# A gated mix of a long convolution and an MLP on one core: the same 1183 operations in another written-out order

## The chip, the cores and the metric

The kernel runs on one core of a Trainium2 chip. The time is device microseconds of one execution of the whole program, weights and activations read from HBM and the result written back to HBM. TensorE (PE) multiplies matrices, VectorE (DVE) and ScalarE (ACT) work on tiles of 128 partitions in SBUF and PSUM, GpSimd (POOL) does small arithmetic and issues DMAs that accumulate, and SyncE (SP) issues the other DMAs. Each engine takes its own instructions in the order in which they were written, and waits at semaphores for the others.

## The reference

One sequence of S = 2048 rows and D = 640 columns in bfloat16; F = 1536. `A_q` is both the query of branch A and the input of branch B.

```python
def _A_ref(q, k, v, shift_k, ssm_k, ssm_D):
    for t in range(ks):                      # 4 taps
        k_shift = k_shift + k_pad[:, t:t + S, :] * shift_k[:, ks - 1 - t]
    kv = k_shift * v
    y = irfft(rfft(kv padded to 2S) * rfft(ssm_k padded to 2S))[:S]
    y = y + kv * ssm_D
    return q * y

def _B_ref(x, w1, w2, w3, w4):
    h = gelu(layernorm(x) @ w1)
    hs = concat(four groups of columns of h, shifted by +1, -1, +2, -2 rows) @ w2
    x1 = x + hs
    return x1 + gelu(layernorm(x1) @ w3) @ w4

x = A_q
g = sigmoid((x * gate_w).sum(-1, keepdims=True))
return g * _A_ref(x, ...) + (1 - g) * _B_ref(x, ...)
```

(Shortened; the padding and the transposes are left out.)

## The kernel before

The kernel is written in two steps. First, functions such as `ln1`, `mm1`, `mm2`, `h_chunk`, `unit` and `final` record operations in the class `Prog` (line 175): each has an index from 0 to 1182, an engine, and the operations that it depends on. One operation can hold several instructions (a group of matmuls into one PSUM tile, a pass with an accumulator). Helpers record them, so the profile shows the helper's line: `mm` (L647) for matmuls, `act` (L637), `tt` (L627), `ts` (L632), `pool_pow` (L815), `Prog.dma` (L238). Second, `schedule` (line 255) puts the operations in the order of the list `SEQUENCE` (line 460), and each engine's and each DMA queue's instructions follow that order. The list `PLACES` (line 521) gives the first PSUM bank of each of 205 PSUM tiles; when a tile opens in a bank, its first operation waits for the operations other than PE's that used the tile before it there. `emit` (line 276) turns the dependences into semaphore waits. Nothing is decided at run time: both lists were written out ahead.

The stages, with the names of the groups that the text uses:

- Start: 15 warm-up matmuls (L675) on a tile that a DVE memset (L671) fills, and 26 fill matmuls (L679) that compute nothing the output needs. `x_load` brings rows of `A_q`; operations 73 to 76 load row tiles 0 to 3. `ln1` takes mean and variance on DVE (L811, L812), raises to the power -1/2 on POOL (L815), applies both on DVE, transposes on PE (L866, row tiles 0 to 7), and copies the transposed tile out of PSUM on ACT.
- `mm1` multiplies by w1 in pieces. ACT applies gelu while it evicts each piece into `hT`. The fifth piece of a chunk holds the last 32 columns of the four shift groups, so it is evicted in four pieces of 32 partitions, at partitions 0, 32, 64 and 96, each with its own shift. `mmg` computes the gate's products, `mm2` multiplies by w2 with the shift in the address, and the residual is added on DVE (L919) or on PE.
- `ln_math` and `ln2` are the second layer norm. For row tiles 4 to 15 the mean, power and the multiply of the two are 128x1 operations on POOL, and ACT applies them. `ln_math-15-16` (operations 580 to 585) belongs to row tile 15; 584 is its power, 585 its multiply, 586 the apply.
- `h_fold` and `h_chunk` transform the filter `ssm_k`, `kv_chunk` makes kv, `x_fwd` transforms it: folded DFTs as matmuls, evicted mostly by ACT. `combine` and `unit` form the spectral products on DVE (products of 128x2560), some of them added by accumulating DMAs on POOL's queue (798, 810, 968, 970 among them).
- `mm3` (w3, gelu on ACT) and `mm4` (w4) finish branch B; 895 to 916 are mm4 of row tiles 8 to 11, of which 897 evicts tile 8.
- `final` runs 16 times, `final-hh-c-q-k` with half of the columns hh: an inverse transform on PE, an ACT copy, a sum and a difference on DVE, a matmul with a flip matrix, an ACT eviction, then two or more DVE operations and the store. Its two row tiles go out in one store of 160 KB for k up to 13 and in two of 80 KB for k = 14 and 15. It is the last work of the kernel.

Of the kernel before, what the change touches and what calls it, by code (L numbers as in the profile page):

```python
# [422 lines left out]
def bass_gated_mix__ssm_conv_h3__mixer_s_mlp__prompt_kernel(  # L423
# [32 lines left out]
    def ps(n, cls):  # L456
# [3 lines left out]
    SEQUENCE = [76, 11, 56, 74, 54, 9, 1, 12, 75, 5, 4, 53, 7, 13, 8, 0, 73, 10, 14, 156, 15, 157, 16, 57, 60, 17, 81,  # L460
# [59 lines left out]

# [645 lines left out]
```

## Time and profile before

| | us |
|---|---|
| median of 3 runs | 231.58 (231.22 to 231.77) |
| profiled execution | 233.02 |
| its span, first to last instruction | 231.2 |
| PE busy | 219.1 (95%) |
| DVE busy | 206.8 (89%) |
| ACT busy | 175.3 (76%) |
| POOL busy | 96.3 (42%) |
| mean granted TensorE clock | 0.993 |

Busy time counts instructions that run, not the semaphores, branches and DMA issues. Weight loads of PE overlap its matmuls. Ends of matmuls are modelled and spans on POOL are rough, so differences of tenths of a microsecond on single POOL rows say little. A wait's releaser is inferred from semaphore events; `A <- B` reads "A waited for B".

### The profile page before, as it was taken

The page shows a single profiled execution, that of the slowest core. Times are in us where ns is not written, and L with a number is a line of the kernel's source. Part 1 is how long each engine was busy: PE and PEld are TensorE (multiplying, and loading weights), DVE is VectorE, ACT ScalarE, POOL GpSimd, SP SyncE. Part 2 cuts the span into 40 slices and gives each one's busy share as a digit, 9 for nine tenths or more (in the row PEclk, how much of TensorE's full clock was granted, in tenths as well). Part 3 has the DMA queues.
Part 4 walks back from the last instruction along what each step waited for, and adds up shares of the span by engine and source line. Part 5 has one row for each costly group of instructions (what it writes and reads, how often), then busy time and mean ns, then how long its engine had stood idle before and what let it go on. Part 6 is the DMA issues. An engine that isn't in the chain of part 4 may idle for free.

```text
span 231.2 us, 3878 instructions
## 1 busy us (share of the span) xinstructions
PE 219.1 (95%) x1437; PEld 127.0 (55%) x1437; DVE 206.8 (89%) x339; ACT 175.3 (76%) x315; POOL 96.3 (42%) x111
## 2 busy tenths in 40 slices
PE   7999999999999999999999999999996999999970
PEld 2588765445445534446764457754574644777640
DVE  4999998979899699599999999968999997996892
ACT  2278999788799879999889863599974389527880
POOL 0344043461233081000086517491399351746880
PEclk9999999999999999999999999999999999999997
DMA  6999999999889989999777999999793999999997
GB/s 171 339 248 288 181 275 128 291 229 216 160 159 269 189 232 215 237 195 216 191 120 120 166 171 263 244 200 152 180 188 65 224 254 196 143 168 127 99 149 127
DMA packets 81007, 45.01 MB, mean 195 GB/s; under 512 B 59976, under 2 KB 75868, under 8 KB 80988
## 3 DMA queue, kind: packets, MB, share of 16 engines
q1 hardware_dynamic: 71560, 31.92, 61.6%
q0 software_dynamic: 9264, 12.78, 37.3%
q8 instruction: 11, 0.18, 0.3%
q10 hardware_dynamic: 164, 0.07, 0.1%
q14 instruction: 8, 0.07, 0.1%
HBM read 14.92 MB, written 6.55 MB: 93 GB/s over the span
## 4 chain that ended last, share of the span: by engine, by line
PE 77%; ACT 11%; POOL 5%; DVE 4%; issue 2%
PE PSall L647 71%; ACT arena L637 10%; DVE arena L627 3%; POOL arena L627 3%; PE PSall L679 2%; PE PSall L675 2%; POOL arena L238 1%; POOL arena L815 1%; ACT PSall L637 1%; PE PSall L866 1%; DVE arena L919 0%; POOL out_dram L238 0%; DVE arena L671 0%; PE PSall L710 0%
## 5 line engine op out<-in xcount | busy, mean ns | idle before, releaser
L647 PE MATMUL PSall<-arena 128*128 128x320 bf16 (+4 forms) x1354 | 206.1, 310 | 4.9 <-ACT arena L637 3.0
L627 DVE TENSOR_TENSOR arena<-arena 128x2560 bf16<-128x2560 bf16 (+6 forms) x198 | 161.1, 864 | 11.4 <-ACT arena L637 9.6
L647 PEld LDWEIGHTS PSall<-arena 128*128 128x128 bf16 x1354 | 120.5, 98 | 90.5 <-ACT arena L637 10.3
L637 ACT ACTIVATE arena<-PSall 128x512 bf16<-128x512 f32 (+8 forms) x182 | 106.1, 628 | 26.4 <-PE PSall L647 18.2
L637 ACT ACTIVATE arena<-arena 128x640 bf16<-128x640 bf16 (+4 forms) x75 | 54.2, 744 | 8.5 <-DVE arena L627 5.1
L238 POOL DMA_DIRECT2D out_dram<-arena x28 | 32.6, 1300 | 46.4 <-ACT arena L637 37.9
L627 POOL TENSOR_TENSOR arena<-arena 128x4 bf16<-128x4 bf16 (+3 forms) x26 | 23.2, 915 | 25.2 <-DVE arena L627 24.5
L238 POOL DMA_DIRECT2D arena<-arena x15 | 22.2, 1490 | 23.9 <-DVE arena L627 23.9
L637 ACT ACTIVATE arena<-PSall,arena 128x640 bf16<-128x640 f32 (+1 forms) x32 | 20.4, 654 | 14.4 <-PE PSall L647 14.2
L815 POOL TENSOR_TENSOR arena<-arena 128x1 f32<-128x1 f32 (+2 forms) x17 | 17.9, 1054 | 20.3 <-DVE arena L826 10.8
L632 DVE TENSOR_SCALAR arena<-arena 128x640 bf16<-128x640 bf16 (+3 forms) x45 | 23.3, 544 | 0.7 <-POOL arena L815 0.3
L632 POOL TENSOR_SCALAR arena<-arena 128x2 f32<-128x2 f32 (+4 forms) x21 | 11.9, 571 | 13.4 <-DVE arena L812 6.1
L811 DVE BATCH_NORM_STATS2 arena<-arena 128x6 f32<-128x320 bf16 x32 | 14.6, 473 | 2.3 <-DMA arena<-in_A_q_dram 2.2
L919 DVE SCALAR_TENSOR_TENSOR arena<-PSall,arena 128x640 bf16<-128x640 f32 x12 | 9.8, 823 | 4.6 <-PE PSall L647 4.5
L675 PE MATMUL PSall<-arena 128*128 128x512 bf16 x15 | 5.5, 551 | 1.6 <-DVE arena L671 1.6
L679 PE MATMUL PSall<-arena 128*128 128x512 bf16 x26 | 6.6, 379 | 0.0
L675 PEld LDWEIGHTS PSall<-arena 128*128 128x128 bf16 x15 | 1.9, 134 | 4.7 <-issue 2.8
L866 PE MATMUL PSall<-arena 128*128 128x128 bf16 x40 | 3.4, 220 | 0.2 <-ACT arena L637 0.2
L866 PEld LDWEIGHTS PSall<-arena 128*128 128x128 bf16 x40 | 2.6, 98 | 1.3 <-ACT arena L637 0.4
L812 DVE BATCH_NORM_AGGREGATE arena<-arena 128x2 f32<-128x12 f32 x16 | 3.1, 199 | 0.1
L679 PEld LDWEIGHTS PSall<-arena 128*128 128x128 bf16 x26 | 2.2, 97 | 1.7
L637 ACT ACTIVATE PSall<-PSall 128x640 f32<-128x640 f32 x4 | 2.8, 700 | 0.1
(26 smaller groups left out, 10.5 us busy)
## 6 DMA issues: line engine op xcount, KB each, us to landing
arena<-arena POOLq DMA_DIRECT2D x12, 640.0 KB, 7.4
arena<-in_A_q_dram SPq DMA_DIRECT2D x14, 320.0 KB, 4.3
out_dram<-arena POOLq DMA_DIRECT2D x20, 160.0 KB, 4.5
arena<-in_A_ssm_k_dram SPq DMA_DIRECT2D x5, 512.0 KB, 4.6
arena<-in_B_w_dram SPq DMA_DIRECT2D x4, 480.0 KB, 4.8
out_dram<-arena SPq DMA_DIRECT2D x10, 160.0 KB, 3.7
arena<-in_B_w_dram SPq DMA_DIRECT2D x1, 1152.0 KB, 5.6
out_dram<-arena SPq DMA_DIRECT2D x12, 80.0 KB, 3.3
```

What stands on the lines that cost most here:

```text
L238: fn = lambda e: e.dma_start(out, in_, **kw)
L627: P.op(eng, lambda e: e.tensor_tensor(o, real(a), real(b), op), [a, b], [o], dve_ns(o, [a, b], 2) if eng == "dve" else 500)
L632: P.op(eng, lambda e: e.tensor_scalar(o, real(a), s1, s2, op0=op0, **({} if op1 is None else {"op1": op1})), [a] + aps, [o], dve_ns(o, [a] ...
L637: P.op("act", lambda e: e.activation(real(o), real(a), f, bias=bias, scale=scale, **({"accum_out": accum} if accum is not None else {})), ...
L647: fns.append(lambda e, l=l, r=r, i=i: e.matmul(real(o), l, r, start=(i == 0), stop=(i == last)))
L675: P.op("pe", lambda e: e.matmul(real(pw), warm[:, 0:128], warm[:, 128:640], start=True, stop=True), [warm], [pw], 427.0 if i < 14 else 216.0)
L679: P.op("pe", lambda e: e.matmul(real(pw), warm[:, 0:128], warm[:, 128:640], start=True, stop=True), [warm], [pw], 216.0)
L811: P.op("dve", lambda e, o=o, i=i: e.bn_stats(o, i), [i], [o], 400)
L812: P.op("dve", lambda e: e.bn_aggr(bna[:, t, :], bns[k]), [bns[k]], [bna[:, t, :]], 120)
L815: P.op("pool", lambda g: g.tensor_tensor(o, a, e, ALU.pow), [a, e], [o], dur)
L866: P.op("pe", [lambda e, c=c, pb=pb, xn=xn: e.transpose(real(pb)[:, 128 * c:128 * (c + 1)], xn[:, 128 * c:128 * (c + 1)], ident) for c in r ...
L919: P.op("dve", lambda e: e.scalar_tensor_tensor(x, real(pr), 1.0, x, op0=ALU.mult, op1=ALU.add, accum_out=st[1, 0][:, t:t + 1]), [pr, x], [ ...
```

## The change

The two lists are exchanged for others. No operation is added, removed or altered, and no line number moves. ACT's order has 27 places where an instruction's first output partition differs from that of the one before it, where the old order has 33. The load of row tile 1 (74) is first on SP's queue, with its statistics first on DVE; the old order has row tile 3 first (76), then 1 (74), 2 (75) and 0 (73). Behind them SP's queue now has a piece of w2 (67), the load of the next rows (156, 157), the two halves of w1 (61, then 60) and `shift_k` (55); it had 156, 157, a half of w1 (60), two pieces of w2 (67, 66), a load of rows (217), and then the other half of w1 (61). The fills are spread wider. In `ln_math-15-16`, the power 584 stands further ahead on POOL, and the multiply 585 comes between the accumulating DMAs 968 and 970. mm4 of row tiles 8 to 11 runs in the order 8, 10, 9, 11. The group that ends last is `final-1-1-0-12` (operations 1137 to 1146), where it was the two groups with k = 14 and 15.

```diff
-    SEQUENCE = [76, 11, 56, 74, 54, 9, 1, 12, 75, 5, 4, 53, 7, 13, 8, 0, 73, 10, 14, 156, 15, 157, 16, 57, 60, 17, 81,
-                67, 18, 80, 66, 19, 97, 217, 20, 96, 21, 61, 77, 22, 98, 101, 23, 78, 24, 102, 308, 82, 25, 79, 26,
-                94, 64, 69, 27, 85, 70, 93, 28, 218, 29, 83, 30, 106, 588, 71, 84, 31, 161, 72, 32, 175, 33, 86, 34,
...
-                877, 812, 1025, 967, 1032, 1049, 876, 1037, 878, 889, 969, 580, 968, 1059, 890, 817, 850, 1038, 569,
-                895, 818, 814, 970, 1050, 583, 1022, 971, 1039, 896, 584, 819, 820, 572, 1040, 973, 1060, 913, 585,
-                1061, 972, 1091, 573, 897, 914, 1062, 586, 974, 587, 907, 574, 915, 1063, 975, 942, 898, 575, 901,
...
-                1108, 1115, 1145, 1171, 1109, 1116, 1150, 1146, 1172, 1117, 1151, 1118, 1173, 1152, 1177, 1153, 1174,
-                1178, 1175, 1154, 1179, 1176, 1155, 1180, 1156, 1181, 1182]
+    SEQUENCE = [74, 1, 11, 54, 76, 53, 9, 0, 12, 73, 5, 13, 75, 14, 67, 15, 156, 57, 80, 16, 157, 81, 17, 56, 61, 96,
+                18, 60, 97, 19, 77, 55, 20, 94, 21, 82, 93, 22, 23, 85, 78, 24, 86, 25, 95, 79, 26, 2, 98, 27, 83, 90,
+                28, 29, 64, 3, 99, 101, 69, 30, 7, 162, 102, 70, 31, 217, 91, 158, 308, 71, 84, 32, 92, 106, 33, 588,
...
+                848, 580, 741, 1091, 808, 875, 743, 849, 571, 869, 582, 865, 802, 856, 1030, 804, 1018, 801, 866, 810,
+                815, 803, 740, 871, 816, 878, 870, 862, 891, 876, 583, 966, 1068, 911, 584, 1048, 1024, 872, 1049,
...
+                968, 969, 882, 1038, 890, 585, 814, 1053, 1092, 973, 888, 1070, 1054, 1093, 1069, 971, 895, 970, 569,
+                1094, 572, 974, 573, 1071, 896, 1072, 1039, 1073, 574, 972, 947, 907, 586, 1074, 977, 587, 959, 901,
+                897, 1040, 942, 975, 575, 898, 902, 576, 976, 850, 913, 903, 1057, 868, 960, 985, 1035, 914, 948, 983,
...
+                1138, 1104, 1118, 1173, 1166, 1105, 1139, 1177, 1106, 1174, 1178, 1107, 1175, 1140, 1179, 1176, 1108,
+                1141, 1109, 1180, 1142, 1181, 1143, 1182, 1144, 1145, 1146]
...
-    PLACES = [0, 7, 2, 1, 1, 3, 4, 4, 5, 6, 2, 1, 0, 5, 6, 3, 7, 5, 5, 7, 0, 4, 7, 6, 1, 3, 7, 2, 6, 0, 4, 2, 7, 4, 6,
...
+    PLACES = [0, 1, 6, 3, 2, 1, 7, 4, 7, 3, 3, 5, 6, 5, 4, 5, 6, 7, 1, 1, 1, 1, 1, 2, 2, 5, 6, 6, 3, 5, 4, 4, 0, 7, 2,
...
```

112 rows, old and new, of tables (PLACES, SEQUENCE) are left out of this document.

## The prediction, made before the changed kernel was run

> **What bounds the kernel now.** I read the page's list of engines first, then the busy time by stage, then PE's waits, then the chain.
>
> ```profile
> span 231.2 us, 3878 instructions
> PE 219.1 (95%) x1437; PEld 127.0 (55%) x1437; DVE 206.8 (89%) x339; ACT 175.3 (76%) x315; POOL 96.3 (42%) x111
> ```
>
> The profiled execution took 233.02 us, 1.8 us outside its span, and 1.4 us over the median of 231.58. I sum against the profiled execution and carry the difference to the median. TensorE (PE) is busy for 95% of the span, so an order that saves time has to shorten PE's 12 us of pauses. VectorE (DVE) at 89% leaves it little room. The same, by stage (columns: window, PE, weight loads, DVE, ScalarE (ACT), GpSimd (POOL), granted clock, DMA share, GB/s):
>
> ```profile
> 0.00:12.00 12.00, 10.42 (x52) 4.61 (x53) 8.62 (x37) 3.25 (x6) 2.49 (x8) 1.00 0.87 259
> 12.00:40.00 28.00, 27.47 (x296) 20.81 (x295) 26.90 (x68) 25.80 (x67) 8.88 (x18) 1.00 1.11 223
> 40.00:60.00 20.00, 19.20 (x118) 9.31 (x116) 18.40 (x35) 16.54 (x22) 7.33 (x10) 1.00 1.08 237
> 60.00:100.00 40.00, 39.94 (x218) 18.88 (x219) 34.13 (x55) 35.52 (x58) 11.45 (x19) 1.00 0.96 210
> 100.00:135.00 35.00, 35.00 (x201) 19.31 (x200) 34.77 (x33) 31.22 (x53) 11.64 (x10) 1.00 0.91 166
> 135.00:180.00 45.00, 42.87 (x279) 26.98 (x277) 41.91 (x46) 30.65 (x55) 27.95 (x23) 1.00 0.99 183
> 180.00:215.00 35.00, 35.00 (x224) 21.74 (x223) 31.04 (x36) 22.55 (x41) 17.68 (x18) 1.00 1.02 181
> 215.00:232.00 17.00, 9.17 (x62) 5.31 (x59) 10.99 (x36) 9.76 (x18) 8.89 (x8) 0.88 0.95 124
> ```
>
> PE is short of its window by 1.6 us in the first, 0.5 and 0.8 in the next two, 2.1 in 135 to 180, and 7.8 in the last. A busy PE can also run slowly behind ACT: 12 to 40 us has ACT and DVE nearly full beside it. PE's waits by what it waited for (total, times, longest), then pieces of the chain (start, length) and ACT's forms (count | sum, mean ns | idle before):
>
> ```profile
> PE PSall L647 <- ACT arena L637: 3.0, 3, 2.1
> PE PSall L647 <- DVE arena L627: 1.4, 2, 0.8
> ```
>
> ```profile
> 18.09 1.38 ACT arena L637 x5
> ...
> 19.50 0.38 ACT arena L637
> 19.87 0.01 issue
> 19.89 0.38 ACT arena L637
> ...
> 33.41 10.79 PE PSall L647 x60
> ```
>
> ```profile
> L637 ACT ACTIVATE arena<-PSall 32x256 bf16<-32x256 f32 x16 | 6.0, 375 | 0.3
> L637 ACT ACTIVATE arena<-PSall 128x640 bf16<-128x640 bf16 x8 | 5.7, 707 | 2.8 <-PE PSall L866 2.7
> L637 ACT ACTIVATE arena<-PSall 128x128 bf16<-128x128 f32 x16 | 3.8, 280 | 1.1 <-PE PSall L647 1.0
> ```
>
> From 18.09 to 33.41 us the chain runs on ACT alone: there the evictions set the pace.
>
> **The change, part by part.** No operation is added or removed; each engine's queue is reordered, and some PSUM tiles change banks.
>
> (1) *Fewer changes of first partition on ACT.* The chain's first row is four 128x128 evictions and one 128x640 copy, all starting at partition 0: alone 4 x 0.280 + 0.707 = 1.83 us, in a row 1.38, so each of the four joints overlaps by 0.11 us. The 32x256 pieces, which go to partitions 96, 32, 0 in turn, follow one another without overlap (0.375 mean, 0.38 in the chain, then 0.01 of issue). A change of the first output partition costs about 0.12 us. The old list has 33 such changes on ACT and the new one 27: 6 x 0.12 = 0.7 us of ACT's time, nearly all between 12 and 40 us, where it is on the path.
>
> The Trainium skill ("ScalarE: Activation LUTs", the section that prices the ACTIVATE instruction) says that back-to-back ACTIVATEs overlap by about 93 ns, with no condition on partitions. By that alone part 1 would be worth nothing; the rows agree with its size (0.11) but not for the 32x256 pieces, and the rows decide.
>
> (2) *The first tile alone.* Row tile 1 is loaded first on SP's queue; its statistics, POOL's power, the apply and its five transposes go ahead of the other three tiles' instead of in step with them. Fill matmuls are spread between, and the memset for the ones goes ahead of DVE's memset for the warm-up.
>
> ```profile
> 1.58 5.53 PE L675 MATMUL PSall<-arena 128*128 128x512 bf16 x15 [1.58 <-DVE arena L671]
> 9.52 0.70 ACT L637 ACTIVATE arena<-PSall 128x640 bf16<-128x640 bf16 x1 [0.99 <-PE PSall L866]
> 3.88 1.68 DVE L811 BATCH_NORM_STATS2 arena<-arena 128x6 f32<-128x320 bf16 x4 [1.77 <-DMA arena<-in_A_q_dram]
> ```
>
> ACT's first copy started at 9.52 us, behind DVE's statistics of two tiles (four from 3.88 in 1.68 us). With two ahead, 0.84 us of DVE drop out, so the copy starts at about 8.6. The memset swap delays the warm-up by some 0.1. So ACT's stage starts some 0.8 earlier; with the 0.7 of part 1 that is 1.5, a little over the 1.3 that PE is short of its windows between 12 and 60 us (0.5 + 0.8). But the half of w1 that is loaded first now comes behind a piece of w2 in SP's queue, so I take -0.9, with ends -1.5 and +0.3.
>
> (3) *33 to 100 us.* I added up, by the means of the forms, ACT's work queued up to each eviction, and PE's work queued up to the matmul that needs it. At 72 us the tightest pair of the old order stands at ACT 12.2 us behind PE's sum; in the new one the matmul of h_chunk-2 (372) reuses the bank that the eviction 407 of h_chunk-3 empties, and the distance is 10.8. In x_fwd-2 it goes from 13.9 to 12.9. ACT's queue is thus 1.0 to 1.4 us tighter in a stretch with 35.52 of 40 us busy and no slack in the old order (PE short by 0.06). Against this stands its earlier start relative to PE. I take +0.8; ends 0 (it hides) and +2.3 (the tightest pair in full, and the other beside it).
>
> (4) *135 to 180 us.* The rows, in order of engine:
>
> ```profile
> 168.58 2.17 POOL L815 TENSOR_TENSOR arena<-arena 128x1 f32<-128x1 f32 x1
> 170.83 5.91 POOL L627 TENSOR_TENSOR arena<-arena 128x1 f32<-128x1 f32 x1
> ```
>
> ```profile
> 176.78 0.92 ACT L637 ACTIVATE arena<-arena 128x640 bf16<-128x640 bf16 x1 [3.22 <-POOL arena L627]
> 177.60 0.77 ACT L637 ACTIVATE arena<-PSall,arena 128x640 bf16<-128x640 f32 x1
> ```
>
> ```profile
> 178.43 2.75 PE L647 MATMUL PSall<-arena 128*128 128x320 bf16 x19 [2.13 <-ACT arena L637]
> ```
>
> The one-element multiply of the last layer norm (585, `ln_math` of tile 15) took 5.91 us on POOL; its apply (586) waited for it on ACT; the eviction behind that apply freed the bank of an mm4 tile, and PE stood 2.13 us. In the new order the power (584) comes earlier, the multiply directly behind the accumulate DMA 968 with DMA 970 after it, and mm4 runs in the order 8, 10, 9, 11. With the DMAs 850 and 970 no longer ahead of it the multiply starts near 169 instead of 170.83; if it lasts 5.91 again, 586 and the eviction (897) are done near 176.8, and PE asks for that bank, by the sum of its work, at 178.4 to 178.9. The stall goes: -2.1. Against it: 970 lands later for DVE, and ACT copies 803 and 804 stand ahead of three mm3-2 evictions, behind a DVE product that waits for DMA 798. What replaced it on DVE was this wait for ACT:
>
> ```profile
> 153.44 5.38 DVE L627 TENSOR_TENSOR arena<-arena 128x320 bf16<-128x320 bf16 x9 [1.94 <-ACT arena L637]
> ```
>
> That hole is filled by other products, and a smaller one opens ahead of PE's final-0-2 (1048): +0.1 to +1.0, I take 0.8. Net -1.3; ends -2.1 and +1.0 (stall kept, new hole in full).
>
> (5) *180 to 215 us.* PE is full (35.00 of 35). DVE's sum of work ahead of final-0-0 (1086) is 0.95 us larger against PE's, and DVE ended half a microsecond before PE asked for it, so the half beyond is given back: +0.4; ends 0 and +1.3 (all that part 4 won).
>
> (6) *The end.*
>
> ```profile
> 224.53 0.31 PE L647 MATMUL PSall<-arena 128*128 128x320 bf16 x1 [0.84 <-DVE arena L627]
> 225.44 0.31 PE L647 MATMUL PSall<-arena 128*128 128x320 bf16 x1 [0.60 <-DVE arena L627]
> 226.57 0.94 SPq L238 DMA_DIRECT2D out_dram<-arena  x2
> ```
>
> ```profile
> out_dram<-arena SPq DMA_DIRECT2D x10, 160.0 KB, 3.7
> out_dram<-arena SPq DMA_DIRECT2D x12, 80.0 KB, 3.3
> ```
>
> The last group is now final-1-1-0-12: two row blocks in one 160 KB store instead of two of 80 KB. The store lands 0.4 later (3.7 against 3.3): +0.4, ends 0 and +0.8 (twice that, the second half of the arithmetic no longer overlapping it).
>
> Sum: -0.9 + 0.8 - 1.3 + 0.4 + 0.4 = -0.6, that is 232.4 for a profiled execution, and 231.0 for the median.
>
> **The rivals.**
> *ACT falls behind (slower).* In 33 to 100 us the distances of part 3 count in full, 1.4 for the bank of 407 and 0.9 for x_fwd-2, while part 2 wins nothing because that half of w1 arrives late: 0 + 2.3 - 1.3 + 0.4 + 0.4 = +1.8, 233.4. Parts 4 to 6 sum to -0.5, so it decides once part 3 costs about 1.0 us more than part 2 wins. For it: the tight sums. Against: of the 3.0 us that PE waited for ACT in the old trace, all but the 2.1 near 178 us came in two waits, 0.9 together.
>
> *The multiply stays long.* It ran all its 5.91 us beside a row of DVE products without a pause, and no other 128x1 multiply took so long:
>
> ```profile
> 170.30 15.17 DVE L627 TENSOR_TENSOR arena<-arena 128x320 bf16<-128x320 bf16 x14
> ```
>
> ```profile
> L627 POOL TENSOR_TENSOR arena<-arena 128x1 f32<-128x1 f32 x8 | 12.9, 1680 | 0.2
> ```
>
> If DVE's row keeps it waiting, its length is set by DVE's order, and beyond 7.5 us (5.91 plus the slack of 1.6) every microsecond is PE's again. Three products more (15.17 / 14 = 1.08 us each) make 9.1 us: 1.6 of the stall come back, and DMA 970, now queued behind it, lands later for DVE by as much, of which I charge a quarter: part 4 becomes -1.3 + 1.6 + 0.4 = +0.7, the sum +1.4, 233.0. For it: the one row. Against: the other seven multiplies took (12.9 - 5.9) / 7 = 1.0 us on average.
>
> The Trainium skill ("SBUF — State Buffer", on the shared port pair) states such a rule: an exclusive lock, which a DVE operation with two SBUF inputs holds against a GpSimd operation that reads SBUF. The one long case of this trace agrees with it; the seven short ones do not decide.
>
> *All is kept.* ACT hides part 3 and DVE part 5: -0.9 - 1.3 + 0.4 = -1.8, 229.8. For it: PE's sum of work is unchanged and PE follows whatever opens. Against: DVE at 89%.
>
> *Nothing moves.* What PE wins by 180 us, DVE takes back at final-0-0 and the end: part 5 at +1.0: 231.6.
>
> **How the numbers follow.** 0.2% is 0.46 us, about what a measurement of this kernel can tell from no change. My forecast (231.0, own range 230.2 to 232.2): 0.35, of which 0.23 faster, 0.09 the same and 0.03 slower by its upper edge. All kept: 0.18. Nothing moves: 0.07, the same. ACT behind: 0.28. The multiply: 0.12. Faster 0.23 + 0.18 = 0.41; same 0.09 + 0.07 = 0.16; slower 0.03 + 0.28 + 0.12 = 0.43. The range runs from 229.2 (all kept, with part 2 at its end of -1.5) to 233.9 (ACT behind plus half a microsecond of the stall kept).
>
> **What the changed kernel's profile would show.** Part 1: the ACT pieces of the chain end before 33 us, with fewer 0.01 issues between. Part 2: ACT's first copy near 8.6 us. Part 3: PE's waits for ACT between 60 and 100 us, above 0.1 in sum. Part 4: no wait of PE near 178 us, and the multiply's length. Part 5: PE's wait for DVE near 205 us. Part 6: the last store issued near 226.2 us, of 160 KB. I am wrong if PE's busy share between 33 and 100 us falls by over 2 us, or if POOL's multiply lasts over 7.5 us.

## The result and the profile after

The changed kernel is faster by a little: the ratio of its time to the old one's is 0.9908, 95% interval 0.9884 to 0.9932, which is 2.1 us of 231.4. Two of its four executions (232.8 and 234.6 us) and one of seven in a second set (235.6) were slower than the fastest of their set by 1.5% and more, as was one of the old kernel's 77 (235.2), and are left out of the ratios, so that these and not the median of 231.08 are the result; what slowed them no profile shows. The second set of executions (`a_again`) gave 0.9945 (0.992 to 0.997), 1.3 us. I take the gain to be between the two. In the second set the new order's other times also scatter more than the old one's: 228.8 to 230.7 us against 230.7 to 231.9 (one of 232.7 apart).

The changed kernel's page, list of engines:

```profile
span 227.5 us, 3881 instructions
PE 217.7 (96%) x1437; PEld 128.5 (56%) x1437; DVE 205.8 (90%) x339; ACT 175.5 (77%) x315; POOL 96.1 (42%) x111
```

The span is 3.7 us shorter than that of the old profile, more than the times differ. A second profile of the old kernel (below, `b_again`) has a span of 229.1, so 2.1 of the 231.2 belonged to that one execution. Busy time by stage, first the second profile of the old kernel, then the changed kernel; columns as in the prediction:

```profile
12.00:40.00 28.00, 27.40 (x295) 20.62 (x293) 26.90 (x68) 25.80 (x67) 9.03 (x19) 1.00 1.10 228
40.00:60.00 20.00, 19.20 (x117) 9.31 (x115) 18.39 (x35) 16.56 (x22) 7.47 (x10) 1.00 1.06 233
135.00:180.00 45.00, 45.00 (x295) 28.69 (x294) 41.89 (x46) 32.14 (x58) 24.78 (x23) 1.00 1.07 194
```

```profile
0.00:12.00 12.00, 9.83 (x53) 4.35 (x53) 8.41 (x36) 3.40 (x8) 2.44 (x8) 1.00 0.81 231
12.00:40.00 28.00, 27.75 (x287) 20.96 (x288) 26.86 (x67) 25.15 (x67) 9.35 (x17) 1.00 1.10 243
40.00:60.00 20.00, 20.00 (x128) 10.56 (x126) 19.31 (x38) 17.94 (x28) 7.39 (x13) 1.00 1.10 218
60.00:100.00 40.00, 40.00 (x222) 19.52 (x220) 35.20 (x56) 36.81 (x57) 8.60 (x15) 1.00 1.03 226
135.00:180.00 45.00, 45.00 (x296) 28.74 (x294) 42.60 (x47) 32.56 (x56) 29.11 (x24) 1.00 1.01 188
```

PE no longer pauses between 40 and 60 us (20.00 of 20 against 19.20). Between 135 and 180 both are full: the pause near 178 us is not in the second profile of the old kernel either. PE's waits, old kernel (second profile), then changed kernel:

```profile
PE PSall L647 <- DVE arena L627: 1.4, 2, 0.8
PE PSall L647 <- ACT arena L637: 0.9, 2, 0.6
PE PSall L866 <- DVE arena L632: 0.3, 1, 0.3
```

```profile
PE PSall L675 <- DVE arena L671: 1.7, 1, 1.7
PE PSall L647 <- DVE arena L627: 1.4, 3, 0.9
PE PSall L647 <- DMA arena<-in_B_w_dram: 0.7, 1, 0.7
```

PE waits for ACT no more, but for a load of w1. The chain of the changed kernel says the same (start, length); it no longer runs on ACT from 18 to 33 us:

```profile
4.58 7.51 DMA arena<-in_B_w_dram
12.09 0.14 issue
12.23 0.44 PE PSall L647 x5
...
29.23 182.58 PE PSall L647 x1133
```

A busy PE can be a slow one, so I also took the starts of all matmuls. A fill of 512 columns starts every 0.216 us when nothing holds it; a stage's loss is the time between its starts less that interval in proportion to the columns, good to a few tenths of a microsecond. In us, summed over each stage:

| stage | old, profile of the prediction | old, second | new | new, second |
|---|---|---|---|---|
| to 15 us | 2.3 | 2.1 | 3.6 | 3.0 |
| 15 to 60 | 3.4 | 3.6 | 1.1 | 1.1 |
| 60 to 100 | 1.7 | 1.9 | 1.0 | 1.0 |
| 100 to 215 | 2.2 | 0.0 | 0.0 | 0.0 |
| 215 to the last matmul | 2.4 | 2.3 | 2.1 | 2.1 |

The new order wins 2.5 us between 15 and 60 and 0.8 between 60 and 100, and pays 0.9 to 1.5 at the start. Both its profiles are of executions at the low end of its times (229.3 and 228.8 us), so the table shows what the order can win, 1.6 and 2.1 us of span against the old kernel's second profile, and not the mean.

### The profile page after: what moved, and what is told of

Read it like the earlier page. It is cut to its first block, busy times and chain, and to the rows that moved or that the text cites. A ratio compares the mean times of both kernels' runs of the same rounds, so it can differ in the third digit from the quotient of the medians.

```text
span 227.5 us, 3881 instructions
## 1 busy us (share of the span) xinstructions
PE 217.7 (96%) x1437; PEld 128.5 (56%) x1437; DVE 205.8 (90%) x339; ACT 175.5 (77%) x315; POOL 96.1 (42%) x111
## 4 chain that ended last, share of the span: by engine, by line
PE 88%; DVE 4%; DMA 3%; SPq 2%; ACT 1%; issue 1%
PE PSall L647 86%; DVE arena L627 4%; DMA arena<-in_B_w_dram 3%; SPq L238 2%; PE PSall L679 1%; ACT arena L637 1%; PE PSall L866 1%
## 5 line engine op out<-in xcount | busy, mean ns | idle before, releaser
L647 PE MATMUL PSall<-arena 128*128 128x320 bf16 (+5 forms) x1354 | 205.8, 310 | 2.1 <-DVE arena L627 1.4
L647 PEld LDWEIGHTS PSall<-arena 128*128 128x128 bf16 (+1 forms) x1354 | 122.1, 98 | 85.8 <-issue 6.4
L637 ACT ACTIVATE arena<-PSall 128x512 bf16<-128x512 f32 (+7 forms) x182 | 105.4, 626 | 26.1 <-PE PSall L647 18.2
L637 ACT ACTIVATE arena<-arena 128x640 bf16<-128x640 bf16 (+5 forms) x75 | 53.9, 740 | 9.2 <-DVE arena L627 8.2
L815 POOL TENSOR_TENSOR arena<-arena 128x1 f32<-128x1 f32 (+2 forms) x17 | 22.6, 1338 | 45.4 <-DVE arena L826 37.7
L238 POOL DMA_DIRECT2D arena<-arena x15 | 19.1, 1332 | 18.8 <-DVE arena L627 14.8
L627 POOL TENSOR_TENSOR arena<-arena 128x4 bf16<-128x4 bf16 (+3 forms) x26 | 15.5, 606 | 22.2 <-DVE arena L627 19.4
L632 POOL TENSOR_SCALAR arena<-arena 128x2 f32<-128x2 f32 (+4 forms) x21 | 14.4, 689 | 19.9 <-DVE arena L627 9.5
L675 PE MATMUL PSall<-arena 128*128 128x512 bf16 x15 | 5.8, 574 | 1.7 <-DVE arena L671 1.7
L679 PE MATMUL PSall<-arena 128*128 128x512 bf16 x26 | 7.4, 379 | 0.0
L675 PEld LDWEIGHTS PSall<-arena 128*128 128x128 bf16 x15 | 2.0, 139 | 5.1 <-issue 3.2
L866 PEld LDWEIGHTS PSall<-arena 128*128 128x128 bf16 x40 | 2.7, 98 | 0.5
L679 PEld LDWEIGHTS PSall<-arena 128*128 128x128 bf16 x26 | 2.3, 97 | 1.1
```

Source lines behind the costliest of these rows:

```text
L238: fn = lambda e: e.dma_start(out, in_, **kw)
L627: P.op(eng, lambda e: e.tensor_tensor(o, real(a), real(b), op), [a, b], [o], dve_ns(o, [a, b], 2) if eng == "dve" else 500)
L632: P.op(eng, lambda e: e.tensor_scalar(o, real(a), s1, s2, op0=op0, **({} if op1 is None else {"op1": op1})), [a] + aps, [o], dve_ns(o, [a] ...
L637: P.op("act", lambda e: e.activation(real(o), real(a), f, bias=bias, scale=scale, **({"accum_out": accum} if accum is not None else {})), ...
L647: fns.append(lambda e, l=l, r=r, i=i: e.matmul(real(o), l, r, start=(i == 0), stop=(i == last)))
L675: P.op("pe", lambda e: e.matmul(real(pw), warm[:, 0:128], warm[:, 128:640], start=True, stop=True), [warm], [pw], 427.0 if i < 14 else 216.0)
```

## The experiments

In the diffs, `old` and `new` stand for the lists of the two kernels. In mixed orders each PSUM tile has its bank from the list that its first operation was taken from.

**Both kernels once more.** `a_again` is the changed kernel, `b_again` the old one, with no edit.

> The changed kernel unaltered, for a second profile and more times beside the old kernel. Theory A (the new order itself removes PE's pauses, 3.45 us lost in 20 to 60 us down to about 1.1, and the 2.3 us near 178 us gone): ratio near 0.991, no pause of PE for ACT between 12 and 210 us again. Theory B (the profiled execution of the old order was 1.5 us over its median because its multiply 585 happened to last 5.9 us, so half the difference between the two traces is chance): ratio near 0.995 and a different length of the power 584, which took 6.33 us in the first trace.

> The old kernel unaltered, for a second profile. In the profiled execution on which the prediction rests, POOL's multiply 585 took 5.91 us and PE then stood 2.13 us near 178 us; in three profiles whose order is the old one in that stretch (the regrouped kernel and the two with a new first part) it took about 1.3 us and PE did not stand. Theory (the long multiply belongs to that execution): multiply under 2.2 us, no pause of PE near 178 us, span near 229.3 us. Rival (the old kernel as a whole has it): 5.9 us, pause, span near 231.

`a_again`: 0.9945 (0.992 to 0.997), span 227.0. `b_again`: 230.92 us, span 229.1. POOL's queue in `b_again`, and then the same in the changed kernel:

```profile
168.73 2.12 POOL L815 TENSOR_TENSOR arena<-arena 128x1 f32<-128x1 f32 x1
170.93 1.27 POOL L627 TENSOR_TENSOR arena<-arena 128x1 f32<-128x1 f32 x1
172.16 1.80 POOL L815 TENSOR_TENSOR arena<-arena 128x1 f32<-128x1 f32 x1
```

```profile
154.83 6.33 POOL L815 TENSOR_TENSOR arena<-arena 128x1 f32<-128x1 f32 x1 [1.68 <-DVE arena L826]
164.97 2.01 POOL L627 TENSOR_TENSOR arena<-arena 128x1 f32<-128x1 f32 x1
```

The multiply 585 that took 5.91 us took 1.27 here, in the same order, and PE ran through; it also took 1.27 in `b_group`, `ab190` and `ab590` below, whose order is the old one there. Theory B of `a_again` held for the old profile: its pause belonged to that one execution. Theory A's other half held as well: PE had no wait for ACT in `a_again`. Theory B's other sign did not come: in the new order the power 584 is the long one, and it took 6.33 us again in `a_again`, as in all eight profiles that have this order there. Two DVE rows of the changed kernel stand beside it:

```profile
154.66 6.06 DVE L627 TENSOR_TENSOR arena<-arena 128x2560 bf16<-128x2560 bf16 x7
161.71 6.64 DVE L627 TENSOR_TENSOR arena<-arena 128x640 bf16<-128x640 bf16 x7 [0.98 <-ACT arena L637]
```

The power began 0.17 us after a row of seven DVE products and ended at 161.16, 0.44 us after that row's end, in DVE's first break. It is needed by 585 at 164.97, and PE lost nothing in this stretch.

**The multiply on DVE.** The old order, with 585 on DVE.

```diff
-            tt(s[4], s[2], s[5], ALU.mult, eng="pool")
+            tt(s[4], s[2], s[5], ALU.mult, eng="dve" if a == 15 else "pool")
```

> The old order with one operation on another engine: the multiply of mean and power of row tile 15 (585) is done by DVE, where it is 0.15 us, instead of POOL, where it took 5.91 us beside DVE's products. Theory A (the multiply is held up by DVE's products and holds up ACT's apply and so an eviction and PE): PE's pause of 2.3 us near 178 us goes, and the time falls by 1 to 2.3 us (ratio 0.990 to 0.996). Rival (the pause was chance of the one profiled execution, or ACT or DVE takes it back by 210 us): ratio within 0.998 to 1.002.

1.0015 (1.0004 to 1.0027): the rival. There was no pause to remove in most executions, and the time rose by 0.3 us.

**ACT's pieces regrouped.** The old order with seven operations moved (148 ahead of 126; 128 and 149 together ahead of 147; 198 ahead of 196; 187 and 208 ahead of 209; 251 ahead of 253). Two of the places:

```diff
-                146, 129, 127, 233, 138, 126, 130, 224, 148, 230,
+                146, 129, 127, 233, 138, 148, 126, 130, 224, 230,
...
-                198, 195, 216, 266, 205, 229, 593, 438, 199, 335, 196, 203, 193,
+                195, 216, 266, 205, 229, 593, 438, 199, 335, 198, 196, 203, 193,
```

> The old order with only ScalarE's pieces of 32 partitions regrouped by first partition between 18 and 52 us (seven of its evictions moved by a few places): 26 changes of the first output partition instead of 33; all else stays. Theory A (each change costs 0.117 us of ACT's time, which is on the chain from 18 to 33 us): 7 x 0.117 = 0.8 us of ACT, the time falls by 0.4 to 0.8 us (ratio 0.9965 to 0.998). Rival (the pieces that are moved hold PSUM banks longer or PE waits for others): within 0.2 us.

0.9975 (0.9965 to 0.9985), 0.6 us: theory A. The stage from 12 to 40 us, and PE's waits for ACT:

```profile
12.00:40.00 28.00, 28.00 (x301) 21.43 (x300) 27.72 (x69) 25.79 (x68) 10.06 (x19) 1.00 1.11 227
PE PSall L647 <- ACT arena L637: 1.2, 1, 1.2
```

PE is full to 40 us (28.00 against 27.40) and then waits 1.2 us once, where the old kernel had waited 0.6 there: part of the gain is given back at the next eviction. In the two first traces, ACT's back-to-back instructions overlap by 0.10 us on average where the first output partition stays (over 200 pairs in each) and leave 0.01 to 0.02 us between them where it changes (32 and 24 pairs). It is the change and not the smaller pieces: in three and four pairs one piece of 32 partitions follows another with the same first partition, and they overlap by 0.09 us.

**New up to 20 us, then old.**

```diff
-    SEQUENCE = old
+    SEQUENCE = new[:190] + [i for i in old if i not in set(new[:190])]
```

> The first 190 operations in the new order (all of the start, to about 20 us), the rest in the old order. Theory A (the start alone wins nothing: PE waits for the half of w1 instead, and the new order's gain comes later): within 0.4 us of the old kernel. Rival (as predicted, the earlier first tile is worth about 0.8 us): ratio 0.996 or less.

0.9983 (0.9971 to 0.9994), 0.4 us, between the two, and at theory A's bound. PE's loss is 3.0 us to 15 us (old: 2.1) and 2.3 from 15 to 60 (old: 3.6): the start pays 0.9 and the stage behind it wins 1.3.

**New up to 86 us, then old; and the reverse.**

```diff
-    SEQUENCE = old
+    SEQUENCE = new[:590] + [i for i in old if i not in set(new[:590])]
```

```diff
-    SEQUENCE = old
+    SEQUENCE = old[:590] + [i for i in new if i not in set(old[:590])]
```

> The first 590 operations in the new order (to about 86 us), the rest in the old order. Theory A (the gain is made before 90 us, where PE lost 5.2 us between 20 and 100 in the old order and 2.2 in the new one): 1.3 to 2.2 us faster than the old kernel (ratio 0.990 to 0.9945). Rival (the gain is made behind 135 us): ratio over 0.997.

> The counterpart: the first 590 operations in the old order, the rest in the new one. Theory A (nothing is won behind 90 us, as the pause near 178 us belonged to one execution of the old order, and the new end costs some): between 0 and 0.6 us slower than the old kernel. Rival (the multiply's pause is in most executions and the new order removes it): 1 to 2 us faster.

`ab590`: 0.9952 (0.9929 to 0.9974), 1.1 us, a little under theory A's range, whose sign and stage it bears out. `ba590`: 1.0071 (1.0056 to 1.0085), 1.6 us slower, more than expected. Its trace shows the price of the seam, the place where one list gives way to the other:

```profile
95.98 2.33 PE L647 MATMUL PSall<-arena 128*128 128x512 bf16 x10 [1.11 <-ACT arena L637]
```

This wait, where x_fwd-2 of the new list meets ACT's queue of the old one, is in neither kernel; behind it PE runs full to the end stage, as in both. So the second half of the new order wins nothing that can be seen. The two halves' ratios do not add up to the whole's because of such seams.

**w1 first.** The new order, with the halves of w1 moved up on SP's queue.

```diff
-    SEQUENCE = [..., 73, 5, 13, 75, 14, 67, 15, 156, 57, 80, 16, 157, 81, 17, 56, 61, 96, 18, 60, 97, ...
+    SEQUENCE = [..., 73, 5, 13, 75, 61, 60, 14, 67, 15, 156, 57, 80, 16, 157, 81, 17, 56, 96, 18, 97, ...
```

> The new order with the two halves of w1 (61, 60) ahead of the piece of w2 and of the next load of rows on SP's queue. In the changed kernel the chain starts with that queue and the landing of 60 at 12.09 us, 7.51 us after its issue, and PE waits 0.83 us for it. Theory A (the order of the loads is what the start now waits for): 60 lands before 10.5 us, the wait goes, the time falls by 0.5 to 0.8 us against the changed kernel. Rival (the rows 156 and 157 come later by the same amount and DVE's statistics for the next tiles hold PE instead, or the fills behind it take up the time): within 0.3 us of the changed kernel.

0.9972 (0.9953 to 0.9991) against 0.9945 for the changed kernel in the same set: not faster, and by these ratios 0.6 us slower, more than the rival's 0.3, though the intervals overlap. The rival's cause is what the trace shows. PE's waits, then DVE's rows:

```profile
PE PSall L866 <- DVE arena L632: 2.6, 3, 1.7
```

```profile
11.02 0.89 DVE L811 BATCH_NORM_STATS2 arena<-arena 128x6 f32<-128x320 bf16 x2 [2.42 <-DMA arena<-in_A_q_dram]
11.82 0.43 DVE L632 TENSOR_SCALAR arena<-arena 128x640 bf16<-128x640 bf16 x1
```

DVE's statistics of the next rows (158, 162) now wait 2.42 us for their load, and the apply 106 of a first row stands behind them in DVE's queue. So both were moved:

```diff
-    SEQUENCE = [..., 75, 14, 67, 15, 156, ..., 157, 81, 17, 56, 61, 96, 18, 60, 97, ...
-                ..., 7, 162, 102, ..., 91, 158, 308, ..., 106, 33, 588, 34, 10, 176, 100, ..., 123, 103, 107, ...
+    SEQUENCE = [..., 75, 61, 60, 14, 15, 156, ..., 157, 67, 81, 17, 56, 96, 18, 97, ...
+                ..., 7, 102, ..., 91, 308, ..., 106, 33, 588, 34, 10, 100, ..., 123, 103, 162, 158, 176, 107, ...
```

> The new order with the two halves of w1 on SP's queue ahead of the next rows (156, 157) and of the piece of w2, as tried before, and now DVE's statistics of those rows (158, 162, 176) behind the three applies of the first rows (106, 87, 103), so that no apply stands behind a wait for the later rows. Theory A (the start waits for whichever load is last, and DVE's order passed that wait on to PE in the earlier trial): PE's 1.9 us wait for the apply 106 goes, both halves land before 10.5 us, and the time is 0.5 to 1.2 us under the changed kernel (ratio 0.985 to 0.990). Rival (the loads' total sets the start, and the later rows now hold up the next tiles): within 0.4 us of the changed kernel.

0.9904 (0.9877 to 0.993), 229.0 us. Against `a_w1first` this is 1.6 us less, and the intervals lie apart; the apply 106, which had ended at 12.26 us, ends at 9.45. Two things were changed for that, DVE's order and the place of the piece of w2, and no run has one alone. That it is faster than the changed kernel is not shown: its ratio is under that kernel's second set (0.9945), level with its first (0.9908), and the span of its profile, 227.4 us, is between that kernel's two (227.0 and 227.5). No wait of PE for w1 is left:

```profile
PE PSall L675 <- DVE arena L671: 1.7, 1, 1.7
PE PSall L647 <- DVE arena L627: 1.4, 3, 0.9
PE PSall L866 <- DVE arena L632: 0.4, 1, 0.4
```

**Without the late fills.** The new order without the 15 fills behind the first product of w1, and the same with the starts moved as above. These fills compute nothing the output needs.

```diff
-                ..., 173, 38, 105, 39, 161, ..., 40, ..., 41, ..., 52, 195, ...
+                ..., 173, 105, 161, ..., 195, ...
...
             o = ops[i]
+            o.preds = {u: w for u, w in o.preds.items() if u not in range(38, 53)}
```

> The new order without the 15 fill matmuls (38 to 52) that come after the first product of w1; they compute nothing the output needs. From 12.23 to 211.8 us the chain of the changed kernel runs on PE with no pause, and 15 fills of 0.216 us lie in it, 3.2 us. Theory A (PE sets the pace there, so they cost what they take): 1.5 to 3 us less than the changed kernel. Rival (ACT's evictions are just behind PE, and the fills stand where PE would have waited): the chain goes to ACT between 12 and 33 us as in the old order, and the time stays within 0.5 us.

> The same without the 15 late fill matmuls. Theory (ACT's evictions, the filter's loads and DVE stand right behind the fills, as the earlier trial without them showed): within 0.4 us of the kernel with the fills. Rival (with the earlier start ACT keeps up without them): another 0.5 us or more less.

0.9938 (0.9918 to 0.9958) and 0.9912 (0.9883 to 0.994): each within 0.2 us of its counterpart with the fills, less than their intervals of 0.5 us and more either way can tell; the rival in the first and the theory in the second. The 3.2 us of fills leave PE's queue, and the traces have waits in their place, PE's rows of the first:

```profile
38.34 12.42 PE L647 MATMUL PSall<-arena 128*128 128x512 bf16 x66 [1.33 <-DMA arena<-arena]
51.50 1.52 PE L647 MATMUL PSall<-arena 128*128 128x512 bf16 x24 [0.74 <-DVE arena L919]
```

**The old end.**

```diff
-    SEQUENCE = old
+    SEQUENCE = new[:1100] + [i for i in old if i not in set(new[:1100])]
```

> The first 1100 operations in the new order (to about 210 us), the rest in the old order, so that the end is the old one: two stores of 80 KB. Prediction's part 6 (the new end costs 0.4 us): 0.3 to 0.5 us less from the last flip's wait to the end of the span than in the new order, and the time that much under the changed kernel's. Rival (the end is set by DVE's last products in either order): the same within 0.2 us.

0.9998 (0.9981 to 1.0015), slower than the changed kernel, so neither expectation. Ahead of the seam the two orders have done the same operations but for five, and of those that the new one has left over one is DVE's. Behind it DVE pauses four times between 213 and 222 us (1.2, 1.1, 0.8 and 0.5 us; the new order has one of 0.6 there, and one of 0.4 ahead of its last two products), and PE's flips wait:

```profile
PE PSall L647 <- DVE arena L627: 3.6, 5, 1.3
PE PSall L647 <- DVE arena L919: 0.8, 1, 0.8
PE PSall L647 <- DMA arena<-arena: 0.5, 1, 0.5
```

PE's loss behind 215 us is 4.6 us in this trace, against 2.1 in the new order. The seam hides what was to be measured.

The last two rows, at 38 and 52 us, are those of the kernel without late fills. Here they came with the fills, and up to 210 us this order is the new one, whose own two profiles do not have them. This execution took 232.97 us, 1.5 over the median of its run, and the two profiles without late fills are of executions 0.8 and 1.0 over theirs. So these waits come and go with the execution, and how much of them the missing fills caused is open. At 38 us PE waits for a DMA (319) that SP issues at 34.6 us here, at 34.9 and 34.2 in the two without late fills, and at 33.7 and 32.5 in the two profiles of the new order. It lands 3.3 to 4.4 us after its issue in the three traces where PE waited for it. The new order first needs it at 38.4 and 37.8; the old one issues it at 29.7 and needs it at 37.9. By these numbers the new order has up to two microseconds to spare for this load, where the old one had about four. Its times may scatter for this reason, but no run tests it.

## Why the prediction was right or wrong

The forecast was 231.0 us, -0.6; the measured change is -1.3 and -2.1 in two sets. The sign and the wide range held, the size was too small (both sets lie at or below 230.2, the lower edge of my own range), and the terms did not come out as set.

(1) *Fewer changes on ACT*: right. In the old order the regrouping alone is worth 0.6 us, for seven changes, where I charged 0.7 for six. In the new order no run has it alone: ACT's busy time from 12 to 40 us fell by 0.65 (25.80 to 25.15), but the two windows do not hold the same instructions, and over the whole span it did not fall (175.3 and 175.5).

(2) *The first tile alone*: wrong, on PE's side. DVE came out as I had it: row tile 1's apply ends at 8.00 us, 0.8 ahead of the first apply of the old kernel (8.79 in its second profile). But I let the copy start at 8.6 us, and it started at 9.20 (9.34 there), since its transposes stand behind warm-ups and fills in PE's queue:

```profile
8.28 0.60 PE L679 MATMUL PSall<-arena 128*128 128x512 bf16 x2
8.72 0.44 PE L866 MATMUL PSall<-arena 128*128 128x128 bf16 x5
```

The warm-ups start every 0.427 us at first and every 0.216 later, and between 6 and 13 of these starts are slow in the 14 profiles, so PE comes free sooner or later. In `ab590`, which has the same start, 7 were slow: the transposes started at 8.00, right behind the apply, and the copy at 8.49. No run takes these early fills out. Then PE waited for the half of w1 that lands at 12.09. Taken with part 1, -0.9 was expected up to 60 us; the losses to 60 us fell by 1.0 to 1.6 (5.7 to 4.7 and 4.1), with the start dearer by 0.9 to 1.5 and the stage behind it better by 2.5. Of these 2.5, `ab190` has 1.3 from the first 190 operations and the regrouping is worth 0.6 in the old order; the two may overlap, and what makes the rest is not taken apart.

(3) *33 to 100 us*: the step that failed. I charged +0.8 for ACT's tighter queue; between 60 and 100 us PE has no wait for ACT in either kernel, and its loss there fell by 0.8. The tight pair exists: in the changed kernel the eviction 407 ends at 70.21 us and the matmul 372 starts at 70.34. Where PE did wait for ACT, its matmul started 0.055 us after the eviction's end, so 0.08 us was to spare. What I overlooked is ACT's own waits in this stretch, from 60 to 100 us, in the second profile of the old kernel and in the changed one:

```profile
ACT arena L637 <- PE PSall L647: 4.1, 8, 1.2
```

```profile
ACT arena L637 <- PE PSall L647: 2.8, 5, 0.9
```

I read "PE short by 0.06" as a stage without slack. ACT waited 4.1 us for PE there. In the new order it has 1.3 us more work in this stretch (36.81 against 35.52) and waits 1.3 us less; that these are the 1.0 to 1.4 that I had summed up fits, but is not shown by itself. The mixed order that ends at 86 us shows this half alone to carry 1.1 us.

(4) *135 to 180 us*: the mechanism exists, its price was that of one execution. -2.1 of the term was a pause that a second profile of the old kernel and the kernel with the multiply on DVE do not show. The profiled execution took 1.4 us more than the median, and I carried that difference over instead of asking which row it sat in. The +0.8 for DVE's hole was wrong too: PE lost 0.0 there in the new order. Sum of this part 0 instead of -1.3.

(5) *180 to 215 us*: +0.4 was charged, 0.0 measured (PE full, no wait near 205 us).

(6) *The end*: the time from the last flip's matmul to the end of the span is 6.2 us in both profiles of the new order (220.77 to 227.0, 221.30 to 227.5) and 5.8 in the old one (223.29 to 229.1): +0.4, as charged, less 0.2 of smaller waits ahead of it. The run that was to test this alone could not, but the other profiles agree: 5.7 to 5.9 us in six that end as the old order does (6.1 in `ab1100`, the seventh), 6.1 to 6.4 in the seven that end as the new one does. About half is the store, as I had it; the other half is DVE, whose last product ends 1.9 us after that matmul's start instead of 1.7.

Against the second profile of the old kernel the parts come to -1.0 and -1.6 (parts 1 and 2), -0.9 (part 3), 0 (parts 4 and 5) and +0.2 (part 6). So two errors cancelled in part: a gain of 1.3 in part 4 that was not there, and costs of 0.8 and 0.4 in parts 3 and 5 that did not come, part 3 winning 0.9 besides. That the sum had the right sign was in part luck. The nearest case was the rival that all is kept (229.8); its reason, that PE follows whatever opens, is what the profile shows, but its number too holds the 1.3 of part 4 and nothing for part 3, and came near by luck.

*The multiply stays long* happened in another place: the long operation is now the power 584 (6.33 us), 3.8 us ahead of its need. *ACT falls behind* did not happen.

The Trainium skill ("SBUF — State Buffer", on the shared port pair) has a DVE operation with two SBUF inputs hold an exclusive lock against a GpSimd operation that reads SBUF. The 6.33 us row that ends in DVE's first break agrees; the multiply 585 at 5.91 and 1.27 us beside the same DVE row shows that a GpSimd operation sometimes gets in between two products, and no run here settles when. The rule of "ScalarE: Activation LUTs" (the section that prices ACTIVATE) that back-to-back instructions overlap by about 93 ns fits where the first output partition stays (0.10 us) and not where it changes.

## What to carry to other kernels

Before a profile's longest wait becomes a term of a forecast, look whether the profiled execution is slower than the median by about as much; if so, the wait may be that execution's own, and a second profile settles it. The same holds for the trace of an experiment, as `ab1100` shows. A queue that gets tighter by a microsecond need cost nothing while its engine still waits that long in the same stretch, so look for the slack in that engine's waits, not in the pauses of the engine that it feeds. When a load is moved ahead, move also what waits for the load that it displaces: in an in-order queue that wait holds up everything behind it.

## What the runs showed that I had not expected

A POOL operation on 128x1 elements took from 0.2 to 6.3 us, and the same one in the same order 1.27 or 5.91. Removing 3.2 us of fills from a PE that never paused changed the time by 0.2 us, no more than the runs can tell: ACT, a DMA and DVE each stand right behind. And a seam ahead of which the two orders have done the same operations but for six cost 1.6 us (`ba590`), one with five 2.5 us of PE's time in the trace (`ab1100`), so that a half of such an order is worth less apart than in the whole.
